# Three landings instead of two for the last turned V blocks of a decode attention kernel

## The chip, the cores and the metric

The kernel runs on one core of one Trainium2 chip. The metric is the device time of one execution in microseconds (us). The sets of runs below were made on different chips (numbers 14, 1 and 10); each set has its own runs of the kernel before.

## The reference

The reference mixes an attention block over a cached K and V with a small MLP, for one token:

```python
q = (x @ wq)                       # 16 query heads of 256, one token
k = repeat(k_cache, 2, axis=1)     # 8 kv heads, 65536 positions, 256 wide
v = repeat(v_cache, 2, axis=1)
p = softmax(q k^T / 16)
a = concat_heads(p v) @ wo
b = layernorm -> gelu MLP -> ...
out = g * a + (1 - g) * b          # g = sigmoid(sum(x * gate_w))
```

K and V together are 537 MB, and each byte is used once. What follows concerns only the last V block of the last kv head, and the last 0.46 MB of `wo`.

## The kernel before

K and V stream through three large buffers on the queue of the sync engine (SP), 48 steps in all. In each step VectorE transposes K, TensorE computes scores and sums P·V. The last V block (80 groups of 128 positions, here called blocks; each 512 bytes for each of 128 partitions) is treated apart, because nothing can hide what comes after its landing. It is loaded in pieces, each with its own semaphore. The first 56 blocks are summed "upright" like all others. The last 24 are summed "turned": V is the stationary operand, so that the result already lies across the partitions as the output projection needs it, with two short matmuls for each block.

```python
TURN = 24
TAIL = 10
# ... SP queue, at the end of all loads
edges = [0, nlast - TURN - SB, nlast - TURN, nlast - TAIL, nlast]   # 0, 40, 56, 70, 80
s_last = [nc.alloc_semaphore(f"s_last{k}") for k in range(len(edges) - 1)]
for k in range(len(edges) - 1):
    lo, hi = edges[k] * DH, edges[k + 1] * DH
    sp.dma_start(out=vlast[:, lo:hi], in_=src[:, lo:hi]).then_inc(s_last[k], 16)
sp.wait_ge(s_oo, HKV - 1)
for r in range(2):                       # the last output weights, in two halves
    at = (HKV - 1) * 512 + r * DH
    sp.dma_start(out=wo[:, r, :, :]..., in_=A_wo[at:at + DH, :]...).then_inc(s_wl[r], 16)
# ... TensorE and VectorE, at the end
pe.wait_ge(s_last[2], 16)
turned(edges[2], edges[3])
pe.wait_ge(s_last[3], 16)
turned(edges[3], edges[4]).then_inc(s_fp, 1)     # line 781: two matmuls a block
dve.wait_ge(s_fp, 4)
heads().then_inc(s_fd, 1)                        # line 565: scale by gate / denominator
pe.wait_ge(s_fd, 3)
for k in range(4):                               # line 830: 16 output products
    r, cc = divmod(k, 2)
    if cc == 0:
        pe.wait_ge(s_wl[r], 16)                  # first 8 need half 0, last 8 half 1
    for a in range(4):
        ins = pe.matmul(acc4[32 * a:32 * a + 1, 0:DQ], lhsT=oT[...], rhs=wo[:, r, cc, ...], ...)
dve.tensor_copy(out=res[0:97, :], in_=acc4[0:97, 0:DQ])   # line 837: the cast
# ... and the store
```

Note the order on the queue: all V pieces first, then the two halves of the weights.

The softmax here doesn't subtract the row's maximum and nothing guards it: scores larger than these inputs give would overflow.

## Time and profile before

| | before |
|---|---|
| time, median of the first 3 runs | 1265.35 us (1265.33 to 1265.42) |
| span of the profiled run | 1263.6 us |
| TensorE / VectorE busy | 57% / 54% |
| moved by DMA | 544 MB, 431 GB/s |

Two lines of the page of the kernel before: the busy share of the DMA engines in 40 equal slices, in tenths, and the packets of the whole run.

```profile
DMA  9999999999999999999999999999999999999998
DMA packets 15944, 544.30 MB, mean 431 GB/s; under 512 B 1856, under 2 KB 2114, under 8 KB 3394
```

The DMA engines are at nine tenths or more in every slice but the last. TensorE and VectorE, at 57% and 54%, follow them.

The chain of waits of the kernel before, its end (start in us, length in us, what):

```profile
1227.99 31.01 DMA kbuf<-in_A_v_cache_dram
...
1259.05 0.71 PE misc L781 x20
...
1259.78 0.17 DVE oT L565
...
1260.00 0.59 PE acc L830 x15
...
1260.61 0.27 DVE res L837
```

Read alone, this says: the last V piece lands at 1259.00, then 20 matmuls, then the rest. Whatever shortens the 20 matmuls seems to shorten the kernel.

The DMA issues of the tail of the kernel before, with size and median time from issue to landing:

```profile
kbuf<-in_A_v_cache_dram SPq DMA_DIRECT2D x1, 640.0 KB, 31.0
wo<-in_A_wo_dram SPq DMA_DIRECT2D x2, 224.0 KB, 31.2
```

The two halves of the weights were issued at 1228.47 and 1228.94 and took 31.2 us: the second landed at 1260.16. That is later than the start of the output products, 1260.00, in the chain above. The next view shows what this means. It is the table of stretches of the kernel before for the instructions that touch `wo` (stretch, its length, PE matmuls busy with their count, PE weight loads busy with their count, granted clock, DMA share, GB/s):

```profile
1259.98:1260.10 0.12, 0.10 (x8) 0.10 (x8) 0.50 0.00 0
1260.10:1260.19 0.09, 0.09 (x8) 0.00 (x0) 0.50 0.00 0
1260.19:1260.32 0.13, 0.13 (x16) 0.10 (x8) 0.50 0.00 0
```

The weight-load column counts starts best, since these loads are short. Eight of the 16 output products begin before 1260.10, none between 1260.10 and 1260.19, eight after. The chain merges the two groups into one line and so hides a second thing that ends here: the landing of the second half of the weights.

### The profile page before, as it was taken

The numbers are of one execution on the slowest core, as the hardware profiler recorded it, in microseconds if no ns is written. First come the engines' busy times: TensorE is split into PE (matmuls) and PEld (weight loads), VectorE is DVE, ScalarE is ACT, GpSimd is POOL, SyncE is SP. The second block draws the span as 40 slices with busy tenths as digits, with TensorE's granted clock in tenths as the row PEclk, the third lists the DMA queues.
The fourth block names the chain that finished last, engine by engine and source line by source line (L and its number), as shares of the span: only waits on it lengthen the run. The fifth ranks groups of instructions, "written<-read, shape, count | busy, mean of one in ns | idle before, by whom it ended". The sixth has DMA issues, their size and how long they took to land. (4 is left out here: it accounts for less than half of the span.)

```text
span 1263.6 us, 10684 instructions
## 1 busy us (share of the span) xinstructions
PE 725.8 (57%) x4310; PEld 283.2 (22%) x4310; DVE 680.7 (54%) x489; ACT 50.1 (4%) x127; POOL 78.4 (6%) x111
## 2 busy tenths in 40 slices
PE   4855656466554665556565565555645656466556
PEld 1311222122211222112222222222212222122212
DVE  5745555465644556455555554564545645465544
ACT  0000000000000000000000000000000000000000
POOL 1001010110110101101011011000000000000000
PEclk9887877878887787777877778778877778778887
DMA  9999999999999999999999999999999999999998
GB/s 408 423 436 429 441 437 424 439 433 431 440 435 423 434 433 438 440 430 432 433 429 440 430 436 439 424 435 433 429 447 429 427 441 432 431 439 432 432 436 348
DMA packets 15944, 544.30 MB, mean 431 GB/s; under 512 B 1856, under 2 KB 2114, under 8 KB 3394
## 3 DMA queue, kind: packets, MB, share of 16 engines
q1 hardware_dynamic: 15848, 544.22, 99.7%
q8 instruction: 2, 0.03, 0.0%
q10 hardware_dynamic: 90, 0.01, 0.0%
q14 instruction: 4, 0.03, 0.0%
HBM read 544.22 MB, written 0.00 MB: 431 GB/s over the span
## 5 line engine op out<-in xcount | busy, mean ns | idle before, releaser
L685 PE MATMUL sc<-kT,qw 128*128 128x512 bf16 x2048 | 571.9, 438 | 482.9 <-PEq L681 482.9
L533 DVE STREAM_TRANSPOSE kT<-kbuf 128x2048 f32<-128x2048 f32 x256 | 572.8, 2285 | 334.4 <-DVEq L525 334.4
L685 PEld LDWEIGHTS sc<-kT,qw 128*128 128x128 bf16 x2048 | 210.8, 108 | 842.6 <-issue 689.2
L699 PE MATMUL pv<-vbuf,pT 128*4 128x512 bf16 x2008 | 119.5, 386 | 26.8 <-PEq L727 26.7
L544 DVE TENSOR_TENSOR og<-pv,og 128x512 f32<-128x512 f32 x40 | 27.6, 691 | 98.5 <-DVEq L525 97.6
L632 ACT ACTIVATE p_t<-sc 128x512 bf16<-128x512 f32 x48 | 28.7, 597 | 1191.2 <-PE sc L685 1191.2
L699 PEld LDWEIGHTS pv<-vbuf,pT 128*4 128x4 bf16 x2008 | 46.8, 87 | 96.2 <-issue 49.9
L616 DVE STREAM_TRANSPOSE pT<-p_t 128x512 bf16<-128x512 bf16 x32 | 22.8, 711 | 74.2 <-DVEq L525 74.2
L659 POOL TENSOR_SCALAR t_b<-t_b 128x448 f32<-128x448 f32 x14 | 7.9, 567 | 362.6 <-ACT t_b L641 362.6
L663 POOL TENSOR_SCALAR t_b<-t_b,hw 128x448 f32<-128x448 f32 x14 | 9.0, 641 | 331.5 <-ACT t_b L649 331.5
L662 POOL TENSOR_TENSOR t_b<-t_b,u_b 128x448 f32<-128x448 f32 x14 | 15.8, 1129 | 1.2
L667 POOL TENSOR_TENSOR t_b<-t_b,u_b 128x448 f32<-128x448 f32 x14 | 15.8, 1128 | 1.2
L668 POOL TENSOR_TENSOR ymix<-ymix,t_b 128x448 f32<-128x448 f32 x14 | 15.8, 1127 | 1.1
L750 PE MATMUL acc<-wo,oT 128*1 128x448 bf16 x28 | 8.6, 443 | 10.4 <-PEq L748 10.4
L543 DVE COPY og<-pv 128x512 f32<-128x512 f32 x8 | 5.5, 692 | 15.5 <-DVEq L525 15.5
L739 PEld LDWEIGHTS misc<-col_f,og 128*128 128x128 f32 x56 | 13.6, 327 | 0.8
L621 DVE STREAM_TRANSPOSE pT<-p_t 128x512 bf16<-128x512 bf16 x8 | 5.7, 711 | 14.9 <-DVEq L525 14.9
L596 DVE STREAM_TRANSPOSE pT<-p_t 128x512 bf16<-128x512 bf16 x8 | 5.7, 712 | 14.2 <-DVEq L525 14.2
L739 PE MATMUL misc<-col_f,og 128*128 128x1 f32 x56 | 12.7, 348 | 0.0
L641 ACT ACTIVATE t_b<-h_bc,b1T,w1T 128x448 f32<-128x448 f32 x14 | 10.5, 748 | 0.0
L655 POOL TENSOR_SCALAR u_b<-h_bc,w1T,b1T 128x448 f32<-128x448 f32 x14 | 10.1, 719 | 4.1 <-DVE hw L429 2.7
L453 PE MATMUL sc<-vbuf,xw 128*128 128x512 bf16 x32 | 9.8, 482 | 0.0
(93 smaller groups left out, 90.3 us busy)
## 6 DMA issues: line engine op xcount, KB each, us to landing
kbuf<-in_A_k_cache_dram SPq DMA_DIRECT2D x32, 5120.0 KB, 33.2
vbuf<-in_A_v_cache_dram SPq DMA_DIRECT2D x31, 5120.0 KB, 20.6
kbuf<-in_A_k_cache_dram SPq DMA_DIRECT2D x16, 6144.0 KB, 35.5
vbuf<-in_A_v_cache_dram SPq DMA_DIRECT2D x16, 6144.0 KB, 23.6
wo<-in_A_wo_dram SPq DMA_DIRECT2D x7, 448.0 KB, 23.6
vbuf<-in_A_wq_dram SPq DMA_DIRECT2D x1, 3072.0 KB, 10.2
kbuf<-in_A_v_cache_dram SPq DMA_DIRECT2D x1, 2560.0 KB, 26.3
kbuf<-in_A_v_cache_dram SPq DMA_DIRECT2D x1, 1024.0 KB, 28.3
```

Source lines behind the costliest of these rows:

```text
L533: dve.transpose(out=kT[b][:].bitcast(FP32), in_=kn[:, s * SB * 128:(s + 1) * SB * 128]).then_inc(s_kt, 1)
L544: return dve.tensor_tensor(out=og[:], in0=pv[:], in1=og[:], op=ALU.add)
L616: dve.transpose(out=pT[:], in_=p_t[:]).then_inc(s_pt, 1)
L632: ins = act.activation(out=p_t[:], in_=sc[:], func=ACT.Exp, scale=scale, accum_out=den[:, c:c + 1])
L641: ins = act.activation(out=t_b[:], in_=h_bc[:], func=ACT.Square, scale=w1T[:, b:b + 1], bias=b1T[:, b:b + 1],)
L655: lambda: pool.tensor_scalar(out=u_b[:], in0=h_bc[:], scalar1=w1T[:, b:b + 1], scalar2=b1T[:, b:b + 1], op0=ALU.mult, op1=ALU.add,),
L662: lambda: pool.tensor_tensor(out=t_b[:], in0=t_b[:], in1=u_b[:], op=ALU.mult),
L667: lambda: pool.tensor_tensor(out=t_b[:], in0=t_b[:], in1=u_b[:], op=ALU.mult),
L668: lambda: pool.tensor_tensor(out=ymix[:], in0=ymix[:], in1=t_b[:], op=ALU.add),
L685: ins = pe.matmul(sc[:], lhsT=qw[:, q, at:at + 128], rhs=kv[:, :, q // 2, :, q % 2], start=(first and q == 0), stop=(last and q == 7), ski ...
L699: ins = pe.matmul(pv[32 * a:32 * a + 4, :], lhsT=pT[:, k, :, ROW0 + s], rhs=vt[:, j * DH:(j + 2) * DH], start=first and k < 4, stop=last a ...
L739: pe.matmul(misc[:, 504 + c:505 + c], lhsT=og2[:].rearrange("p r (q c) -> p c r q", c=4)[:, c], rhs=col_f[:], start=(c == 0), stop=False, ...
```

## The change

The last turned piece of 10 blocks becomes two of 6 and 4. Fewer blocks remain to be summed after the last landing: 8 matmuls instead of 20.

```diff
-TAIL = 10
+TAILS = (10, 4)
@@
-        edges = [0, nlast - TURN - SB, nlast - TURN, nlast - TAIL, nlast]
+        edges = [0, nlast - TURN - SB, nlast - TURN] + [nlast - t for t in TAILS] + [nlast]
@@
-        pe.wait_ge(s_last[2], 16)
-        turned(edges[2], edges[3])
-        pe.wait_ge(s_last[3], 16)
-        turned(edges[3], edges[4]).then_inc(s_fp, 1)
+        for k in range(2, len(edges) - 1):
+            pe.wait_ge(s_last[k], 16)
+            ins = turned(edges[k], edges[k + 1])
+        ins.then_inc(s_fp, 1)
```

## The prediction

> **What bounds the kernel now.** The DMA queue. The 16 DMA engines are at 9 tenths or more in nearly every slice, 431 GB/s over the span, TensorE 57%, VectorE 54%. In the tail (timeline, DMA issues with time to landing) the four pieces of the last V blocks land at 1252.9, 1255.3, 1257.4 and 1259.0 us; behind them on the same queue come the two halves of the last output weights (issued 1228.47 and 1228.90, 31.2 us to landing: 1259.6 and 1260.1-1260.2). After the 1259.0 landing the chain of waits has 20 turned matmuls (line 781) 0.71 us, the head scaling on VectorE 0.17, the output products (line 830) 0.59, the cast 0.27, the store.
>
> **What the change removes.** The last turned piece falls from 10 blocks to 4, so 8 matmuls remain after its landing in place of 20. They follow one another at 26.7 ns: 12 x 26.7 = 0.32 us less. The new middle piece is summed in a gap in which TensorE idles (0.44 us before line 781). By the chain of waits alone: 0.3 us less.
>
> **Why I do not expect that.** The chain of waits shows the output products as one run of 16. The single records show two runs: the first 8 (first half of the weights) start at 1259.996-1260.055, the other 8 at 1260.204-1260.262, and the first of these waits for the semaphore of the second half of the weights, whose last increment came at 1260.16. Without it they would have started by about 1260.10. So the last landing on the queue is already what ends last; finishing the heads earlier only widens the gap between the two runs from 0.15 us to about 0.5 us.
>
> **What it adds.** One more DMA in front of those weights. The packets of one engine follow each other every 192.5 ns for 5120 bytes and 70.5 ns for 1792 bytes, so about 4.8 ns each plus 0.0367 ns per byte (estimate from these two). Rows of 5120 bytes become rows of 3072 and 2048: 8 more packets per engine, 8 x 4.8 = 38 ns, and a semaphore packet of about 10 ns: +0.05 us on the landing of the weights. The added issue on SP, 0.43 us, hides behind 30 us of queued work. The Trainium skill, page "DMA: Bandwidth & Descriptors", section "Queues, rings and completion order", says each engine consumes its ring in order; the landings here, in order of issue, agree.
>
> **Predicted:** 1265.40 us, 0.05 us above before; 8 in 10 between 1265.15 and 1265.70. Faster by over 2%: 0.002; within 2%: 0.996; slower: 0.002.
>
> **What would show it.** Line 781 after the last V landing: 8 matmuls; the last V piece lands at 1259.0-1259.1; head scaling ends near 1259.7 (before 1259.94); first run of line 830 near 1259.75; second run still at 1260.2-1260.3, after the second half of the weights has landed. If the second run moves up to 1259.9, the bound I name is wrong.
>
> **What would make it wrong.** Two of the 16 engines finish about 0.9 us after the rest: on the last weights 14 have incremented by 1259.23, two at 1260.05 and 1260.16. One of these fell back behind a fetch of instructions (16 KB, 0.97 us, at 1256.84). If the changed program makes that fetch fall elsewhere, on the other late engine or outside the tail, the end moves by up to 0.8 us either way. Runs differ by 0.09 us.

## The result, and the profile after

| | before | changed |
|---|---|---|
| time, median | 1265.41 us (1265.33 to 1265.77, 6 runs) | 1265.60 us (1265.40 to 1265.73, 6 runs) |
| span of the profiled run | 1263.6 us | 1263.6 us |
| ratio | | 1.0001, 95% interval 0.9988 to 1.0014 |

The ratio is the mean time of one kernel's runs over that of the other's of the same rounds, so it is not quite the ratio of the medians. A second set of runs (after_again, below) had the medians the other way round, 1265.56 against 1265.66. The times do not resolve the predicted +0.05 us.

The page of the changed kernel, packets:

```profile
DMA packets 16088, 544.30 MB, mean 431 GB/s; under 512 B 1872, under 2 KB 2130, under 8 KB 3538
```

There are 144 packets more: 128 rows and 16 semaphore writes, as one more transfer of 128 partitions over 16 engines should have.

The chain of waits of the changed kernel, its end:

```profile
1229.60 30.53 DMA wo<-in_A_wo_dram
...
1260.17 0.39 PE acc L830 x8
...
1260.58 0.27 DVE res L837
```

V, the turned matmuls and the heads have left the chain. It now goes straight from the landing of the weights at 1260.13 to the last 8 output products.

The timeline of the changed kernel from 1259 us, without the weight loads of line 781 and the store (start, length, engine, line, operation, tiles, count, idle time before it and what ended it):

```profile
1259.07 0.37 PE L781 MATMUL misc<-pT,kbuf 128*128 128x2 bf16 x8 [0.21 <-DMA kbuf<-in_A_v_cache_dram]
1259.48 0.16 DVE L565 TENSOR_TENSOR oT<-misc,rden 128x4 bf16<-128x4 f32 x1 [2.83 <-PE misc L781]
1259.70 0.13 PEld L830 LDWEIGHTS acc<-wo,oT 128*1 128x1 bf16 x8 [0.34 <-DVE oT L565]
1259.73 0.80 PE L830 MATMUL acc<-wo,oT 128*1 128x112 bf16 x16 [0.28 <-DVE oT L565]
1260.17 0.10 PEld L830 LDWEIGHTS acc<-wo,oT 128*1 128x1 bf16 x8 [0.34 <-DMA wo<-in_A_wo_dram]
1260.58 0.27 DVE L837 CAST res<-acc 97x112 bf16<-97x112 f32 x1 [0.94 <-PE acc L830]
```

The scaling of the heads starts at 1259.48 instead of 1259.78: the gain of 0.3 us is real there. The first 8 products start 0.27 us earlier, at 1259.73. The last 8 start at 1260.17 (before: 1260.20), because they wait for the weights. From the start of the first group to that of the second it was 0.21 us and is now 0.45 us (single records). The gain was turned into a wait.

### The profile page after: what moved, and what is told of

It reads as the page before. It is cut to its first block, busy times and chain, and to the rows that moved or that the text cites. A ratio compares the mean times of both kernels' runs of the same rounds, so it can differ in the third digit from the quotient of the medians.

```text
span 1263.6 us, 10685 instructions
## 1 busy us (share of the span) xinstructions
PE 727.0 (58%) x4310; PEld 283.8 (22%) x4310; DVE 680.8 (54%) x489; ACT 50.1 (4%) x127; POOL 78.2 (6%) x111
## 5 line engine op out<-in xcount | busy, mean ns | idle before, releaser
L632 ACT ACTIVATION_READ_ACCUMULATOR p_t<-sc 128x1 f32 x48 | 9.3, 194 | 0.0
```

What stands on the lines that cost most here:

```text
L632: ins = act.activation(out=p_t[:], in_=sc[:], func=ACT.Exp, scale=scale, accum_out=den[:, c:c + 1])
```

## The experiments

Theory A, from the prediction: the end is set by the later of two things, the last V landing with the chain behind it, and the last weight landing with the 8 products and the cast behind it. Rival B: the fewer matmuls do gain 0.3 us, and the added transfer (or something else) takes it back, so the equal time is a sum of two real effects.

Landings move by 0.2 to 0.4 us from profile to profile, so a cast time by itself says little. Each profile is therefore read by its own landings, taken from the single semaphore increments in the trace, 16 for each transfer: V is the 16th increment of the last V piece, W that of the second half of the weights. "Behind last V landing" counts the turned-shape matmuls after V. All are single profiles; times in us.

| kernel | behind last V landing | V | W | cast starts | cast - V | cast - W |
|---|---|---|---|---|---|---|
| before | 20 | 1259.00 | 1260.16 | 1260.61 | 1.61 | 0.45 |
| changed | 8 | 1259.03 | 1260.13 | 1260.58 | 1.56 | 0.45 |
| after_again | 8 | 1259.16 | 1260.27 | 1260.72 | 1.56 | 0.45 |
| nowait_10 | 20 | 1259.18 | (1260.36) | 1260.77 | 1.59 | 0.41 |
| nowait_6_4 | 8 | 1259.15 | (1260.31) | 1260.47 | 1.32 | 0.16 |
| dummy12_10 | 32 | 1258.74 | 1260.14 | 1260.64 | 1.90 | 0.50 |
| dummy12_6_4 | 20 | 1259.02 | 1260.10 | 1260.61 | 1.59 | 0.52 |
| tail_24 | 48 | 1258.90 | 1260.03 | 1261.24 | 2.34 | 1.21 |
| tail_20_4 | 8, but the 40 before them still run | 1258.96 | 1260.15 | 1260.67 | 1.71 | 0.53 |
| tail_fours | 8 | 1258.96 | 1260.14 | 1260.59 | 1.64 | 0.45 |

In brackets: not waited for. By this table V + 1.59 and W + 0.45 tie, with 20 matmuls, when W comes 1.14 us after V. In the three profiles with the transfers of the kernel before (before, nowait_10, dummy12_10) W came 1.16, 1.18 and 1.40 us after V, so by how much the weights would end last there, 0.02 to 0.26 us, moves with the landings.

### Taking the wait for the second half of the weights away (nowait_10, nowait_6_4)

The last 8 products read the first half again. The values are wrong, though within the tolerance of the comparison; the transfers are all still there.

```diff
-            if cc == 0:
+            if cc == 0 and r == 0:
                 pe.wait_ge(s_wl[r], 16)
...
-                    rhs=wo[:, r, cc, ...
+                    rhs=wo[:, 0, cc, ...
...
         pool.wait_ge(s_out, 16)
+        pool.wait_ge(s_wl[1], 16)
```

> The kernel before, but the last 8 output products read the first half of the weights again and do not wait for the second half (wrong result on purpose; the second half is still loaded and is awaited only after the store). Theory A (on record: the landing of the second half of the weights ends last): the two runs of 8 output products close up, the second starts at about 1260.10 instead of 1260.20, the cast about 0.10 us earlier. Rival B (the chain of V matmuls and heads ends last, the weights never bind, and the change's gain was eaten by its extra transfer): the last products start where they did, no change.

> The same edit on the changed kernel. Theory A: the second run of output products follows the first at about 1259.80 instead of 1260.17, so the cast starts near 1260.17 in place of 1260.58, 0.4 us earlier than in the changed kernel and 0.3 us earlier than in nowait_10: with this wait away the change is worth its 0.3 us. Rival B: nothing moves, and nowait_6_4 equals nowait_10.

The chain of waits of nowait_10, its end:

```profile
1259.22 0.71 PE misc L781 x20
...
1260.17 0.57 PE acc L830 x10
...
1260.77 0.28 DVE res L837
```

And of nowait_6_4:

```profile
1259.20 0.40 PE misc L781 x8
...
1259.88 0.57 PE acc L830 x16
...
1260.47 0.27 DVE res L837
```

With the wait away, the changed kernel's cast follows its last V landing (1259.15) by 1.32 us, against 1.59 us in nowait_10 (landing 1259.18). So the change is worth 0.27 us exactly when nothing waits for the weights. With the wait, nowait_6_4 would have had its cast at 1260.31 + 0.45 = 1260.76; it came at 1260.47, 0.29 us earlier. 0.4 was expected. The larger reason for the difference is TensorE's own time: from the first product to the cast it took 0.595 us here, where the expectation had the second group at once behind the first. The smaller one, about 0.04 us, is a further wait: the first group started 0.135 us after the landing of the first half of the weights (1259.74), as it did in the changed kernel (0.136 us), and 0.094 us after the heads, in place of 0.055 us in the kernel before. Rival B has no place for this: the extra transfer is still there in nowait_6_4.

nowait_10 missed what was expected. In the kernel before, from the first product to the cast took 0.617 us with the wait and 0.596 us without. Taking the wait away gains 0.02 us, not 0.10, because TensorE itself takes time over 16 products: without the wait, the second group starts 0.14 us after the first, not 0.10, and its own way to the cast grows from 0.41 to 0.45 us. In this profile the kernel before sat near the point where the two bounds tie.

Times: 1265.55 us and 1265.45 us, before in the same rounds 1265.57 us; 95% intervals of the ratio 0.9982 to 1.0016 and 0.9983 to 1.0016. They resolve nothing.

### Putting the removed matmuls back as dummies (dummy12_10, dummy12_6_4)

Twelve matmuls of the same shape are added behind the last V landing, into unused columns. The result stays correct and the transfers are untouched.

```diff
-        turned(edges[3], edges[4]).then_inc(s_fp, 1)
+        turned(edges[3], edges[4])
+        for jj in range(12):
+            ins = pe.matmul(den_ps[:, 2:4], lhsT=vlast[:, (nlast - 1) * DH:nlast * DH:2],
+                            rhs=pTr[:, 0, :, ROW0], start=True, stop=True, ...)
+        ins.then_inc(s_fp, 1)
```

> The kernel before with 12 more matmuls of the same shape behind the last V landing (into unused columns; result correct), 32 in all. Theory A: the kernel before has almost no slack behind its V chain (0.02 us by the run nowait_10), so the heads and the cast come 12 x 26.7 ns = 0.32 us later, some 1.9 us behind the last V landing in place of 1.6. A rival that only the last weight landing counts: cast unmoved, 0.45 us behind that landing.

> The changed kernel with the same 12 matmuls added behind its last V landing, 20 in all as before the change; result correct. Theory A: the changed kernel has about 0.3 us of slack there, because its last products wait for the second half of the weights, so these 12 cost nothing or up to 0.05 us: cast 0.45 us behind the last weight landing. Rival B (the fewer matmuls did gain 0.3 us and the extra transfer ate it): cast 0.3 us later.

The chain of waits of dummy12_10, its end:

```profile
1258.79 0.68 PE misc L781 x20
1259.47 0.33 PE den_ps L823 x12
...
1259.83 0.17 DVE oT L565
...
1260.64 0.28 DVE res L843
```

The chain of waits of dummy12_6_4, its end:

```profile
1259.07 0.37 PE misc L781 x8
1259.44 0.33 PE den_ps L822 x12
...
1259.80 0.17 DVE oT L565
...
1260.61 0.28 DVE res L842
```

In the changed kernel, 12 more matmuls moved the cast from V + 1.56 to V + 1.59, by 0.03 us, and from W + 0.45 to W + 0.52, by 0.07 us (up to 0.05 us was expected; in this profile W came only 1.07 us after V, and the V chain ended last). In the kernel before, they moved it from V + 1.61 to V + 1.90, by 0.29 us. The same 0.32 us of TensorE work costs nearly all of itself in one kernel and nearly nothing in the other. That is the slack the change made and could not use.

A warning lies in dummy12_10: its cast, at 1260.64, is hardly later than that of before, 1260.61, because its last V piece happened to land at 1258.74 instead of 1259.00. Compared by absolute times, the run would have said that 12 matmuls are free. By time, dummy12_10 had 1265.59 us and dummy12_6_4 1265.39 us, before 1265.66 us.

### Making the V chain long, and two pieces instead of three (tail_24, tail_20_4)

```diff
-TAILS = (10, 4)
+TAILS = ()      # tail_24
+TAILS = (4,)    # tail_20_4
```

> All 24 turned blocks in one last piece (one transfer fewer than before, two fewer than changed); correct result. Theory A (the end is the later of two: last V landing plus its chain, and last weight landing plus 0.45 us; before the two tie): the chain grows by 28 matmuls of 26.7 ns = 0.75 us, less 0.05 us for the transfer saved: cast about 0.7 us after that of before, time about 1266.2. Rival B (the number of matmuls behind the last landing does not matter at all, which the equal times of before and changed would also allow): no change.

> Two pieces of 20 and 4, as many transfers as before; correct result. Theory A: the piece of 20 lands about 0.6 us before the last, its 40 matmuls take 1.07 us and are still running when the last lands, so the heads end about 0.1 us later than before and the cast is about 0.1 us later than before. Rival (only the size of the last piece counts): heads as early as in the changed kernel, the cast with it.

The chain of waits of tail_24, its end:

```profile
1258.95 1.46 PE misc L781 x48
...
1260.43 0.17 DVE oT L565
...
1261.24 0.28 DVE res L837
```

tail_24 took 1266.19 us against 1265.41 us before in the same rounds: 0.78 us more, about 0.7 expected, though the interval of the ratio (0.9990 to 1.0023) still holds 1. Its fastest run, 1266.03 us, is above the slowest of before, 1265.90 us. The cast came 0.63 us after that of before in the profiles. So the matmuls behind a landing do count, as soon as they outlast the weights. This excludes that the V chain never matters.

tail_20_4 shows that small last pieces are not enough: the 40 matmuls of the piece of 20 were still running when the last 4 blocks landed, and the cast came 0.06 us after that of before (0.1 expected). Its time was 1265.52 us, before 1265.41 us.

### Turning the queue's order round (wofirst_10, wofirst_6_4)

```diff
+        (the wait for s_oo and the two loads of wo, unchanged)
         for k in range(len(edges) - 1):
             lo, hi = edges[k] * DH, edges[k + 1] * DH
             sp.dma_start(out=vlast[:, lo:hi], in_=src[:, lo:hi]).then_inc(s_last[k], 16)
-        (the wait for s_oo and the two loads of wo)
```

> The kernel before with the two halves of the last output weights queued ahead of the last V pieces instead of behind them; correct result. Theory A: the queue ends as before, now with V, whose last piece lands at about 1260.2; the whole chain behind V (1.5 us from landing to cast without a wait) is exposed, the cast starts near 1261.7, span and time about 1.0 us longer than before. Rival B (weights do not matter for the end): V lands later by the 0.45 MB put ahead of it as well, so the time also rises by 1 us; this run alone does not tell A from B, its difference to wofirst_6_4 does.

> The changed kernel with the same reordering; correct result. Theory A: with V last on the queue the V chain is the end, and the three pieces are worth what the fewer matmuls after the landing are, 0.32 us less 0.05 us for the extra transfer: cast about 0.27 us earlier than in wofirst_10. Rival B (the extra transfer costs as much as the fewer matmuls save): no difference to wofirst_10.

With V last on the queue, the last V pieces landed at 1260.32 and 1260.21, and the cast came 1.57 and 1.26 us later: 0.31 us less with three pieces. The casts were at 1261.89 and 1261.47. So where V is the last thing on the queue, the change does what it was meant to do. The times, 1266.80 and 1266.78 us, with runs from 1266.28 to 1267.03, show the cost of the order (about 1.2 us over before, 1.0 expected) but do not show the difference between the two. TensorE was still at work on the piece before when the last one of wofirst_10 landed, but its last 20 matmuls started 0.045 us after that landing, as in nowait_10, so the pair can be read like the other two.

The order that puts the weights last is thus the better one. The weights are what V's chain hides behind.

### What an extra transfer costs (tail_fours, tail_ones)

```diff
-TAILS = (10, 4)
+TAILS = (20, 16, 12, 8, 4)            # tail_fours: six turned pieces of 4 blocks
+TAILS = tuple(range(23, 0, -1))       # tail_ones: 24 turned pieces of one block
```

> Six turned pieces of 4 blocks, 8 V transfers and 2 of weights; result correct. A milder form of tail_ones, to measure an extra transfer where the queue should not run dry: the last issue may stall until an earlier transfer is done, as the tenth did there, but long before its data are due. By the estimate of 4.8 ns a packet and 10 ns a semaphore packet, 24 packets and 3 transfers more than the changed kernel: 0.145 us later from the first V landing to the last weight landing. If an extra transfer costs nothing: 0; if the stall matters here too: over 1 us.

> The 24 turned blocks in 24 transfers of one block; correct result. From the estimate of 4.8 ns a packet and 10 ns a semaphore packet, 22 more transfers than before cost each engine 176 x 4.8 + 22 x 10 = 1.07 us: the last weights land about 1.07 us later and span and time rise by about 1.0 us (time near 1266.5). If an extra transfer costs nothing on a full queue, no change; if it costs a fixed 0.4 us, as its issue does, over 8 us.

The last increment of a transfer is that of its slowest engine and jitters. The time between the means of the 16 increments of two transfers hardly does: it agrees within 0.005 us among kernels with equally many transfers (table). From that mean for the first V piece to that mean for the last half of the weights, the single records show:

| kernels with | transfers from the first V piece to the end | us between the means |
|---|---|---|
| tail_24 | 5 | 7.369 |
| before, nowait_10, dummy12_10, tail_20_4 | 6 | 7.410 to 7.415 |
| changed, after_again, nowait_6_4, dummy12_6_4 | 7 | 7.450 to 7.453 |
| tail_fours | 10 | 7.586 |

One more transfer costs 0.040 us (before to changed), 0.044 us (tail_24 to before) and 0.045 us each (changed to tail_fours, 0.134 us for three). The estimates were 0.05 and 0.145 us.

tail_ones took 1269.16 us, 3.75 us more than before (ratio 1.0028, interval 1.0011 to 1.0044), where 1.0 us was expected. The packet costs were not what failed: while the queue was still full, ten of the one-block pieces landed 0.198 us apart in the mean of their increments, and the estimate gives 0.199 us (8 packets of 4.8 + 0.0367 x 512 ns, and 10 ns). What failed was the issue. The lines of the issues of tail_fours (the weights) and of tail_ones (the V pieces): engine, operation, tiles, count, then the shortest, median and longest issue in ns:

```profile
L513 SPq DMA_DIRECT2D wo<-in_A_wo_dram x2: 433/9930/19428, 1231.6 to 1232.1; - x2
```

```profile
L508 SPq DMA_DIRECT2D kbuf<-in_A_v_cache_dram x26: 432/432/19428, 1226.7 to 1260.2; - x26
```

An issue takes 432 ns, but in both kernels the tenth one after the last large V load took 19.4 us. SP was held until about 1252 us, when the transfers ahead were landing. In tail_fours that tenth issue was the last, and its data were not due before 1258, so nothing was lost: its one time was 1265.37 us. In tail_ones 18 more issues stood behind it, at about 0.5 us each, and the queue ran dry. So in this kernel adding pieces was cheap only as long as no issue stalled. The changed kernel has seven such issues, none over 0.44 us. The stall does not go by the number of transfers alone: in wo_k14, below, already the ninth issue took 12.0 us.

### The late DMA engines (wo_k14): inconclusive

```diff
-            sp.dma_start(out=wo[:, r, :, :]..., in_=A_wo[at:at + DH, :]...).then_inc(s_wl[r], 16)
+            for p0, p1 in ((0, 126), (126, 128)):
+                sp.dma_start(out=wo[p0:p1, r, :, :]...,
+                             in_=A_wo[at + 2 * p0:at + 2 * p1, :]...).then_inc(s_wl[r], 16)
...
-                pe.wait_ge(s_wl[r], 16)
+                pe.wait_ge(s_wl[r], 32)
```

> The changed kernel with each half of the last output weights in two transfers, of 126 and of 2 partitions, so that (by the Trainium skill, DMA: Bandwidth & Descriptors, Why a DMA increments its semaphore by 16 and not by 1) the first runs on the 14 lowest engines and the second on the lowest 2; correct result. Two of the 16 engines end 0.9 us after the rest. If both late ones are the two left out, the weights land near 1259.6, the chain behind the last V landing (1259.0) ends last and the cast comes about 0.3 us earlier than in the changed kernel. If a late one is among the 14, the weights land 0.15 to 0.2 us later than in the changed kernel and the cast with them. The number of increments in the records (14 and 2) shows whether the split works as stated.

The kernel got slower (1266.14 us against 1265.41 us). But it did not answer the question, because the packets themselves became slower: many of the 1792-byte packets, 74 ns elsewhere, took 100 to 214 ns between 1257.8 and 1259.8 us (91 of 256; 1 of 256 in the kernel before). The last V piece, which was not changed, landed at 1259.96 instead of 1259.03. The weights landed at 1260.94 and the cast followed 0.45 us later. The records of each half hold 16 increments while its data landed, in place of twice 16, and two more before that, which fits 14 and 2 engines; since both transfers share one semaphore, they do not show which engines these were. Why the packets slowed is open, and so is whether the late engines are among the 14.

### The changed kernel once more (after_again)

> The changed kernel itself once more, for the spread from profile to profile: cast 0.45 us behind the last weight landing, gap between the two runs of output products about 0.45 us, time within 0.3 us of that of before. The landings themselves may move by 0.2 us.

The time from the first group of products to the second was 0.45 us and the cast came 0.45 us after the last weight landing, both as in the first profile. The landings were 0.14 us later. Time 1265.56 us, before 1265.66 us.

## Why the prediction was right

**The time.** 1265.40 us was predicted, in a range of 1265.15 to 1265.70; 1265.60 us was measured at first and 1265.56 us again. The sign of the difference to before is not known from the times, and the hit is partly luck: the medians of before alone moved from 1265.41 to 1265.66 us between the sets of runs, nearly half the width of the range. What supports the prediction is the inside of the traces.

**What is removed: 0.32 us of matmuls.** Right. From the last V landing to the end of the heads' scaling went from 0.94 us to 0.62 us, and the pairs nowait, dummy12 and wofirst each show 0.27 to 0.31 us for the same 12 matmuls.

**Why it does not count: the weights land last.** Right. nowait_6_4 shows the 0.29 us returning when the wait goes, and dummy12_6_4 shows that the removed matmuls could be put back for 0.03 to 0.07 us.

A check on the whole: let the cast start at the later of V + 1.59 + 0.0267 (n - 20) and W + 0.45, with n matmuls behind the last V landing. The 1.59 comes from nowait_10 and the 0.45 from the changed kernel. For dummy12_10 this gives 1258.74 + 1.91 = 1260.65 (measured 1260.64), for dummy12_6_4 1259.02 + 1.59 = 1260.61 (1260.61), for tail_24 1258.90 + 1.59 + 0.75 = 1261.24 (1261.24), for tail_fours 1260.14 + 0.45 = 1260.59 (1260.59). Where the weights came early, it gives 1261.91 for wofirst_10 (1261.89) and 1261.48 for wofirst_6_4 (1261.47). It is 0.05 us short for nowait_6_4, 1260.42 (1260.47), where the first group also waited for the first half of the weights. tail_20_4 is outside the rule, since TensorE was busy at V.

**A part that was wrong.** The prediction said of the kernel before that without the wait the second group "would have started by about 1260.10", so that the weights alone ended last by 0.1 us. nowait_10 measured 0.02 us. In the profile of the kernel before the two bounds were nearly tied; the change moved the kernel off the tie on the side where nothing is gained. The new gap was also over-estimated: from the last start of the first run to the first of the second it grew from 0.15 us to 0.39 us, not to about 0.5, because V landed 0.02 us later and W 0.03 us earlier than before, and the first run was held 0.03 us by the first half of the weights.

**What is added: 0.05 us on the weights.** Nearly right: 0.040 us in the mean over the engines. It is smaller than what the slowest engine's landing varies by from run to run (last weight landings of 1260.03 to 1260.36 us in the table above), so the times cannot show it.

**The risk that was named.** In the ten kernels of the table above, two engines ended 0.6 to 1.0 us after the other 14 on the last weights, and the late fetch of instructions fell between 1256.8 and 1257.5 us. The feared jump of the end by 0.8 us was not seen in them.

## What to carry to other kernels

When several transfers end a kernel, ask of each what it still has behind it when it lands, and compare the sums; shortening the work behind one landing only helps while that sum is the largest. A chain of waits names one path and can merge two groups of instructions that wait for different things, so look at the single starts inside the last line before believing its saving. For effects below the spread of the times, compare each trace by its own landings, and confirm with a pair of runs that removes the suspected bound from both kernels.

## What the Trainium skill lacked or had wrong

- "DMA: Bandwidth & Descriptors" (sections "Queues, rings and completion order" and "Rules for kernel authors") gives no figure for how many transfers an SP queue takes before an issue blocks. "Perfetto Trace Analysis" (section "DMA Instruction — HWDGE (DVE, Sync)") names a descriptor buffer that can fill, without its size. Here nine issues after the last large V load took 0.43 to 2.0 us each and the tenth 19.4 us, in tail_ones and in tail_fours alike; in wo_k14, with the weights in transfers of 126 and 2 partitions, the ninth took 12.0 us. What is counted was not tested.
- "Runtime: NRT & Kernel Launch", section "Instruction fetch mechanics", says of the fetch of a 16 KiB block: "The cost of crossing a 16 KiB boundary is one DMA tail-bump, mostly hidden." The trace agrees on the block (packets of 16384 bytes of the kind "instruction", beside some of 8192), but shows such packets taking 0.97 and 1.17 us among the data transfers of the kernel before. In the kernel before the slowest engine was 0.24 us behind the next-slowest on a K transfer at 26 us, before a fetch at 31.4 us, 0.92 us behind at 40 us, after it, and still 0.92 us behind at 1221 us; the 16th increment, which the kernel waits for, is that of the slowest engine. That the fetch caused this is only inferred from the order in time, and no run here tested it.
- No page says what a transfer cut from a larger one costs on a full queue; "DMA: Bandwidth & Descriptors" (section "Why small descriptors are slow (HBM only)") gives an overhead for each packet only. Here it was 0.040 to 0.045 us for 128 rows, in the mean over the 16 engines.
